# Attention, a gated layer and a soft mixture in fp32r on one core: ring tiles 32 bytes longer, with their data begun 0, 8, 16 or 24 bytes in

## The chip, the core and the metric

The kernel runs on one core of a Trainium2 chip. A core has a matrix engine (TensorE, PE in the rows; PEld is its weight loading), a vector engine (DVE), a scalar engine (ACT), GpSimd (POOL), and the queue of the sync engine (SP) that issues the DMAs. The engines run side by side and meet by semaphores. The metric is the device time of one execution in microseconds; lower is better.

## What is computed

Three layers follow one another on 2304 tokens (4 batches of 576) with 512 features. The reference, cut to what matters:

```
scores = scale * q @ k.T                      # B, H, S, D = 4, 8, 576, 64, causal
a = softmax(scores); local = a @ v
mem_out = (phi(q) @ M_prev) / (phi(q) @ z_prev + 1e-6)
x = g * mem_out + (1 - g) * local             # -> 2304 x 512

g = x @ w_gate; val = x @ w_val               # 512 x 1536 each
x = (silu(g) * val) @ w_out                   # 1536 x 512

P = exp(x @ w_gate2 - max); 8 rounds: rows to sum 1, columns to sum 1, times N/E
out = sum over 8 experts e of P[:, e] * (relu(x @ w1[e]) @ w2[e])   # 512 x 1024, 1024 x 512
```

## The kernel before

All large products are made from fp32 operands that are split in two parts of a reduced format (fp32r): `hi` is the operand copied by ACT into fp32r, `lo` is the operand less `hi`, made by DVE or POOL. A product is then three matmuls into one PSUM bank, hi·hi, hi·lo and lo·hi (`product`, L471 to L477, and the loops around L1133, L1221 and L1298). One of the two operands stands in the array (it is loaded, a LDWEIGHTS of 128 columns) and the other moves through it (256 or 512 columns). Every matmul of these products has a weight load of its own, since the order hi·hi, hi·lo, lo·hi goes through the products one by one. The load of the next matmul runs while the present one streams.

Both parts of an operand lie in one SBUF tile of a ring, `[128, 2, 512]` in fp32r, so 4096 bytes in each partition, `hi` in the first 2048 and `lo` in the second. The rings that hold such tiles, with the role of their tiles in the matmuls:

| stage | ring (name in the rows) | role | made by |
|---|---|---|---|
| gated layer, `moe1` | `xs` | moving | `split_x` L459, `halves23` L844 |
| | `gw` (8192 bytes, two such tiles) | standing | `load_units` L507, later loaded by `stream` L532 from DRAM |
| | `h` (made by `halves` L677) | moving | ACT and DVE, L679 and L680 |
| | `ws` | standing, in parts moving | `load_units`, `stream`, `unit_sums` |
| mixture, `moe2` | `xr` | moving | DMA from DRAM, L1345 |
| | `w1` (`w` in the rows) | standing | `parts` L1028 |
| | `h` (made by `split_h` L1105) | standing | ACT and DVE, L1114 to L1118 |
| | `xl` (ring of the second weights, `w2`) | moving | `parts2` L1032 |
| both | `xl` (small ring of two) | moving | `logits` L555, `parts_of` L581 |

The pool hands out places by size. In the kernel before every one of these tiles begins at a multiple of 32 bytes, and tiles of one ring stand 4096 bytes apart. Read from the built program: all `xr` tiles and all eight `h` tiles of the mixture begin 96 bytes past a multiple of 128, the ten `w1` tiles 64 past one, seven of the nine tiles of the second weights 96 past one and two of them 64. In the gated layer `gw`, `ws`, `h` and eight of eleven `xs` tiles begin 96 past a multiple of 128, three `xs` tiles 64 past.

The gated layer and the mixture use a scheme of seven products in place of eight (sums `S1` to `S4` and `T1` to `T4` of quarter matrices). In the mixture an expert's half (a "unit", 16 of them) is taken through five groups of tokens; for each, `unit_hidden` (L1120, matmuls at L1133: `pc<-xr,w` and `pt<-xr,w`, 256 columns) makes the hidden values and `unit_out` (L1277, matmuls at L1298: `pu<-xl,h` and `pq<-xl,h`, 256 columns) the output. Steps of the two are interleaved by the string "HO" * 7 (L1367), and the weights of the next unit are split beside them (`prepare_unit`). `last_hidden` (L1208, matmuls at L1221) is the short last group of tokens. In the gated layer `half` (L663, `p<-xs,gw`), `second` (L683, `po<-h,ws`) and `unit_gates` go through `product`, at L475 in the rows, mostly with 512 columns.

What sets the order: PE, ACT and DVE work in the order in which the framework's scheduler has put the instructions, and SP issues DMAs in its own order. The one stretch in which the schedule mixes two stages is the end of attention, where `load_units` turns the gated layer's weights into split tiles ahead of time.

A constant tile `ones` (L142) is filled by DVE at the start and used by `sinkhorn` (L958) alone, in the mixture's first unit.

## Time and profile before

| | |
|---|---|
| time, median of 2 runs | 2197.91 us (2197.82 to 2198.01) |
| span of the profiled execution | 2196.1 us, so 1.8 us less than the median |
| PE busy | 2149.0 us, 98% of the span, 15848 matmuls |
| PEld busy | 1960.3 us, 89% |
| DVE busy | 1679.1 us, 76% |
| ACT, POOL busy | 986.9 us (45%), 518.7 us (24%) |
| DMA | 425.77 MB, mean 194 GB/s |

Matmuls of one stream overlap: a matmul is recorded with some 280 ns, but the next one starts some 120 ns after it. So the length of a matmul's record is not its share of PE; the pace is. The pace is read from a row of the timeline that merges n matmuls of one kind: its length, less one matmul's mean length, over n - 1.

### The profile page before, as it was taken

The page shows a single profiled execution, that of the slowest core. Times are in us where ns is not written, and L with a number is a line of the kernel's source. Part 1 is how long each engine was busy: PE and PEld are TensorE (multiplying, and loading weights), DVE is VectorE, ACT ScalarE, POOL GpSimd, SP SyncE. Part 2 cuts the span into 40 slices and gives each one's busy share as a digit, 9 for nine tenths or more (in the row PEclk, how much of TensorE's full clock was granted, in tenths as well). Part 3 has the DMA queues.
Part 4 walks back from the last instruction along what each step waited for, and adds up shares of the span by engine and source line. Part 5 has one row for each costly group of instructions (what it writes and reads, how often), then busy time and mean ns, then how long its engine had stood idle before and what let it go on. Part 6 is the DMA issues. An engine that isn't in the chain of part 4 may idle for free.

```text
span 2196.1 us, 40669 instructions
## 1 busy us (share of the span) xinstructions
PE 2149.0 (98%) x15848; PEld 1960.3 (89%) x15848; DVE 1679.1 (76%) x3195; ACT 986.9 (45%) x1944; POOL 518.7 (24%) x463
## 2 busy tenths in 40 slices
PE   7999998999999899999999999999999999999999
PEld 5666677878888789999999999999999999999999
DVE  8777898675454668788887887878878788787877
ACT  6888733343333324444444444444444444444432
POOL 7766645000010042022120221202212022121100
PEclk9999999999999999999999999999999999999999
DMA  6332487466577836556465564655646556465564
GB/s 212 121 106 68 135 287 263 150 225 206 177 256 248 283 125 240 193 182 214 160 231 202 174 221 157 235 197 170 220 156 232 198 175 219 155 232 201 173 202 154
DMA packets 123359, 425.77 MB, mean 194 GB/s; under 512 B 13600, under 2 KB 13600, under 8 KB 120096
## 3 DMA queue, kind: packets, MB, share of 16 engines
q1 hardware_dynamic: 123168, 423.17, 56.5%
q8 instruction: 126, 2.06, 0.4%
q14 instruction: 65, 0.53, 0.1%
HBM read 374.36 MB, written 48.76 MB: 193 GB/s over the span
## 4 chain that ended last, share of the span: by engine, by line
PE 80%; DVE 8%; DMA 6%; issue 2%; POOL 2%; ACT 2%; SPq 1%; POOLq 0%; DVEq 0%; ACTq 0%
PE pu L1298 16%; PE pc L1133 15%; PE pq L1298 11%; PE pt L1133 11%; PE po L475 5%; PE pt L1221 4%; DMA raw<-w 4%; PE p L475 3%; PE pc L475 3%; PE po L447 2%; PE pt L475 2%; PE pq L475 2%; PE pt L414 2%; PE ps L293 1%; POOL na L504 1%
## 5 line engine op out<-in xcount | busy, mean ns | idle before, releaser
L1298 PE MATMUL pu<-xl,h 128*128 128x256 f32 x3240 | 437.3, 282 | 1.1 <-DVE xacc L1304 1.1
L1133 PE MATMUL pc<-xr,w 128*128 128x256 f32 x3072 | 408.6, 281 | 1.2 <-DVE xacc L838 0.8
L1298 PEld LDWEIGHTS pu<-xl,h 128*128 128x128 f32 x3240 | 408.4, 190 | 1.4 <-issue 1.4
L1133 PEld LDWEIGHTS pc<-xr,w 128*128 128x128 f32 x3072 | 380.8, 188 | 9.0 <-ACT m L1140 6.2
L1298 PE MATMUL pq<-xl,h 128*128 128x256 f32 x2430 | 326.4, 282 | 0.0
L1133 PE MATMUL pt<-xr,w 128*128 128x256 f32 x2304 | 306.4, 281 | 6.7 <-DVE m L1145 6.3
L1298 PEld LDWEIGHTS pq<-xl,h 128*128 128x128 f32 x2430 | 305.8, 190 | 0.1
L1133 PEld LDWEIGHTS pt<-xr,w 128*128 128x128 f32 x2304 | 285.0, 188 | 12.6 <-DVE m L1145 11.4
L1117 ACT CAST h<-m 128x512 fp32r<-128x512 f32 (+1 forms) x345 | 189.3, 557 | 217.6 <-DVE m L1149 208.0
L1304 DVE SCALAR_TENSOR_TENSOR xacc<-pu,Pw,xacc 128x256 f32<-128x256 f32 x540 | 237.9, 477 | 40.1 <-PE pu L1298 38.1
L1304 DVE SCALAR_TENSOR_TENSOR xacc<-pq,Pw,xacc 128x256 f32<-128x256 f32 x405 | 178.7, 478 | 109.9 <-PE pq L1298 109.2
L1149 DVE SCALAR_TENSOR_TENSOR m<-m 128x512 f32<-128x512 f32 x240 | 175.5, 731 | 80.7 <-ACT m L1171 79.2
L1118 DVE TENSOR_TENSOR h<-m,h 128x512 fp32r<-128x512 f32 (+1 forms) x345 | 209.3, 617 | 10.0 <-ACT h L1117 8.6
L1039 POOL TENSOR_TENSOR ws<-raw 128x512 f32<-128x512 f32 x62 | 89.0, 1447 | 520.4 <-DMA raw<-w 231.2
L1114 ACT ACTIVATE h<-m 128x512 fp32r<-128x512 f32 x192 | 121.6, 633 | 173.7 <-DVE m L1145 172.1
L1140 ACT COPY m<-pc 128x512 f32<-128x512 f32 x192 | 112.4, 586 | 186.7 <-PE pc L1133 186.6
L475 PE MATMUL p<-xs,gw 128*128 128x512 f32 (+1 forms) x864 | 172.0, 355 | 7.8 <-DVE hf L660 5.3
L475 PEld LDWEIGHTS p<-xs,gw 128*128 128x128 f32 x864 | 143.4, 189 | 34.4 <-DVE hf L660 6.9
L475 PE MATMUL po<-h,ws 128*128 128x512 f32 x576 | 144.6, 392 | 1.7 <-DVE h L680 1.2
L1026 POOL TENSOR_TENSOR w<-raw,w 128x512 fp32r<-128x512 f32 x17 | 27.5, 1620 | 476.9 <-ACT w L1025 476.9
L1115 DVE SCALAR_TENSOR_TENSOR h<-m,h 128x512 fp32r<-128x512 f32 x192 | 134.4, 700 | 4.5 <-ACT h L1114 4.3
L1145 DVE TENSOR_TENSOR m<-pt,m 128x512 f32<-128x512 f32 x192 | 131.7, 686 | 2.5 <-PE pt L1133 2.5
(244 smaller groups left out, 3004.1 us busy)
## 6 DMA issues: line engine op xcount, KB each, us to landing
xr<-xp SPq DMA_DIRECT2D x480, 512.0 KB, 4.0
raw<-w SPq DMA_DIRECT2D x64, 512.0 KB, 7.2
gw<-kg SPq DMA_DIRECT2D x24, 1024.0 KB, 6.6
graw<-gvo SPq DMA_DIRECT2D x36, 512.0 KB, 4.8
xp<-xl SPq DMA_DIRECT2D x30, 512.0 KB, 3.8
kg<-gw SPq DMA_DIRECT2D x24, 512.0 KB, 4.0
ws<-ko SPq DMA_DIRECT2D x24, 512.0 KB, 4.1
qk<-qkv SPq DMA_DIRECT2D x16, 640.0 KB, 4.1
```

Of the source, the lines that this page charges most:

```text
L475: self.nc.tensor.matmul(out, lhs[a], rhs[b], start=start and n == 0, stop=stop and n == 2, skip_group_check=shared)
L1039: op(q[name], q[a], q[b])
L1114: nc.scalar.activation(hi, src, AF.Relu)
L1115: self.later(1, lambda: nc.vector.scalar_tensor_tensor(lo, src, 0.0, f32(hi), op0=ALU.max, op1=ALU.subtract))
L1117: nc.scalar.copy(hi, src)
L1118: self.later(1, lambda: nc.vector.tensor_sub(lo, src, f32(hi)))
L1133: self.marks[3] = nc.tensor.matmul(out[:, j * HT:(j + 1) * HT], w[:, a, j, k], x[:, b, k], start=start and j + k + n == 0, stop=k + n == 3 ...
L1140: self.marks[1] = nc.scalar.copy(t, src)
L1145: nc.vector.tensor_add(t, a, b)
L1149: relu = lambda out, a, b, op: nc.vector.scalar_tensor_tensor(out, a, 0.0, b, op0=ALU.max, op1=op)
L1298: nc.tensor.matmul(po[:, c], h[a][:, x, j, c * P:(c + 1) * P], w2[b][:, y, j], start=start and c + j + n == 0, stop=j + n == 3, skip_group ...
L1304: self.marks[2] = nc.vector.scalar_tensor_tensor(acc, po[:, c], self.Pw[:, at, e:e + 1], acc, op0=ALU.mult, op1=ALU.add)
```

## The change

A new function `odd(pool, name, by)` gives a tile that is 8 elements (32 bytes) longer, and a view into it that begins `by` elements in. The rings named above take their tiles from it: `xs`, `xl` and the small `xl` ring with `by` 0, `w1` with 4 (16 bytes), `h` of the gated layer with 6 (24 bytes), `h` of the mixture with 2 (8 bytes). `wide` does the same for `gw` with 4 (16 bytes). `xr`, `ws`, `m`, `hf` and `sg` keep their tiles. So a tile of a changed ring begins 0, 8, 16 or 24 bytes past a multiple of 32, and two tiles of a ring stand 4128 bytes apart. What is computed and the tiles' shapes are as before. The tile `ones` (512 bytes) leaves the constants and is filled by POOL in `sinkhorn`'s own pool.

```diff
+def odd(pool, name, by=0):
+
+    return pool.tile([P, 2 * 512 + 8], F32R, name=name)[:, by:by + 2 * 512].rearrange("p (a n) -> p a n", a=2)
...
-        self.ones = c.tile([P, P], F32, name="ones")
-        nc.vector.memset(self.ones, 1.0)
...
-            t = (pool or self.xsp).tile([P, 2, 512], F32R, name="xs")
+            t = odd(pool or self.xsp, "xs")
...
+    def wide(self, pool):
+        t = pool.tile([P, 4 * 512 + 8], F32R, name="gw")[:, 4:4 + 4 * 512]
+        return t.rearrange("p (i a n) -> p i a n", i=2, a=2)
...
-                self.gw[f] = self.gwp.tile([P, 2, 2, 512], F32R, name="gw")
+                self.gw[f] = self.wide(self.gwp)
...
-            t = pool.tile([P, 2, 512], F32R, name="xl")[:, :, 0:m * P]
+            t = odd(pool, "xl")[:, :, 0:m * P]
...
-                t = self.xl.tile([P, 2, 512], F32R, name="xl")
+                t = odd(self.xl, "xl")
...
-                h = hp.tile([P, 2, 512], F32R, name="h")
+                h = odd(hp, "h", 6)
...
-            gws = self.stream(lambda: self.gwp, [P, 2, 2, 512], "gw", self.keptg * 2, 2)
-            wss = self.stream(lambda: wsp0, [P, 2, 512], "ws", self.kepto * 2, 3)
+            gws = self.stream(lambda: self.wide(self.gwp), self.keptg * 2, 2)
+            wss = self.stream(lambda: wsp0.tile([P, 2, 512], F32R, name="ws"), self.kepto * 2, 3)
...
+        ones = pool.tile([P, P], F32, name="ones")
+        nc.gpsimd.memset(ones, 1.0)
...
-            w1[name] = self.w1p.tile([P, 2, 2, HT], F32R, name="w1")
+            w1[name] = odd(self.w1p, "w1", 4).rearrange("p a (j n) -> p a j n", j=2)
...
-            t = self.w2p.tile([P, 2, 512], F32R, name="xl")
+            t = odd(self.w2p, "xl")
...
-        t = self.hp.tile([P, 2, 512], F32R, name="h")[:, :, 0:n]
+        t = odd(self.hp, "h", 2)[:, :, 0:n]
```

PE's instructions, with their waits, stand in the same order before and after. Two places on other engines move.

On POOL, at the border of the gated layer and the mixture's first unit (`xs` is the last split of tokens, `na` an intermediate of the weights' conversion, `ws` here the sums of quarter matrices, `w` the `w1` tiles). Before:

```order
L504 TENSOR_SCALAR na<-na 128x512 x30
L467 TENSOR_TENSOR xs<-xacc,xs 128x256 x2
L1039 TENSOR_TENSOR ws<-raw 128x512 x2
L1039 TENSOR_TENSOR ws<-ws,raw 128x512
L1039 TENSOR_TENSOR ws<-raw,ws 128x512
L1026 TENSOR_TENSOR w_6944<-raw,w_6944 128x512
```

and after:

```order
L507 TENSOR_SCALAR na<-na 128x512 x29
L470 TENSOR_TENSOR xs<-xacc,xs 128x256 x2
L969 MEMSET ones 128x128
L1049 TENSOR_TENSOR ws<-raw 128x512 x2
L1049 TENSOR_TENSOR ws<-ws,raw 128x512
L1049 TENSOR_TENSOR ws<-raw,ws 128x512
```

The fill of `ones` now stands on POOL ahead of the first unit's sums; DVE had it as its first instruction.

On DVE, at the end of attention (`gw` is the low part of a weight tile, `T` a transposed piece of attention, `xs` a split of tokens). Before:

```order
L528 TENSOR_TENSOR gw<-nb,gw 128x512
L394 TENSOR_TENSOR Z<-pt,Z 128x512
L394 TENSOR_TENSOR F<-pt,F 128x512
L528 TENSOR_TENSOR gw<-nb,gw 128x512
L488 TENSOR_SCALAR na<-na 128x512
L489 SCALAR_TENSOR_TENSOR na<-graw,na 128x512
L388 COPY xacc<-pt 128x64
L467 TENSOR_TENSOR xs<-xacc,xs 128x512
```

and after:

```order
L535 TENSOR_TENSOR gw<-nb,gw 128x512
L397 TENSOR_TENSOR Z<-pt,Z 128x512
L397 TENSOR_TENSOR F<-pt,F 128x512
L491 TENSOR_SCALAR na<-na 128x512
L492 SCALAR_TENSOR_TENSOR na<-graw,na 128x512
L470 TENSOR_TENSOR xs<-xacc,xs 128x512
L391 COPY xacc<-pt 128x64
L494 TENSOR_SCALAR nb<-na 128x512
```

Here one `gw` subtraction moves some rows down and the first `xs` split comes ahead of a copy. Such swaps go on through `load_units`, on ACT and SP too; behind it the order is as before on every engine.

## Rows read from the trace of the kernel before

**Rows 1.** The page: busy time, slices of the span, chain by engine.
```profile
PE 2149.0 (98%) x15848; PEld 1960.3 (89%) x15848; DVE 1679.1 (76%) x3195; ACT 986.9 (45%) x1944; POOL 518.7 (24%) x463
...
PEclk9999999999999999999999999999999999999999
...
PE 80%; DVE 8%; DMA 6%; issue 2%; POOL 2%; ACT 2%; SPq 1%; POOLq 0%; DVEq 0%; ACTq 0%
```

**Rows 2.** Windows: stretch, sum, busy of each engine, granted clock, DMA share, GB/s.
```profile
610.00:700.00 90.00, 86.56 (x571) 78.06 (x570) 40.98 (x70) 27.11 (x55) 9.32 (x6) 1.00 0.74 264
...
1000.00:1250.00 250.00, 249.76 (x2094) 247.94 (x2093) 200.60 (x384) 107.23 (x187) 47.38 (x31) 1.00 0.61 205
```

**Rows 3.** Whom PE waited for: total us, times, longest.
```profile
PE ps L339 <- ACT KH L254: 7.1, 1, 7.1
PE pt L1133 <- DVE m L1145: 6.3, 10, 1.3
```

**Rows 4.** Timeline of PE in the mixture: start, length, line, operation, count.
```profile
1378.04 1.57 PE L1133 MATMUL pc<-xr,w 128*128 128x256 f32 x12
1379.44 1.60 PE L1298 MATMUL pu<-xl,h 128*128 128x256 f32 x12
```

**Rows 5.** Timeline of PE in the gated layer, and in attention.
```profile
422.99 11.04 PE L475 MATMUL po<-h,ws 128*128 128x512 f32 x48
...
701.71 3.03 PE L475 MATMUL pp<-h,ws 128*128 128x256 f32 x24
```
```profile
18.07 1.56 PE L220 MATMUL po<-mask 128*128 128x128 bf16 x25
```

**Rows 6.** PE's groups by form: count, busy us, mean ns, idle before.
```profile
L1298 PE MATMUL pu<-xl,h 128*128 128x256 f32 x3240 | 437.3, 282 | 1.1 <-DVE xacc L1304 1.1
L1133 PE MATMUL pc<-xr,w 128*128 128x256 f32 x3072 | 408.6, 281 | 1.2 <-DVE xacc L838 0.8 <-ACT m L1140 0.3
L1298 PE MATMUL pq<-xl,h 128*128 128x256 f32 x2430 | 326.4, 282 | 0.0
L1133 PE MATMUL pt<-xr,w 128*128 128x256 f32 x2304 | 306.4, 281 | 6.7 <-DVE m L1145 6.3 <-DMA xr<-xp 0.2
...
L475 PE MATMUL po<-h,ws 128*128 128x512 f32 x576 | 144.6, 392 | 1.7 <-DVE h L680 1.2 <-ACT h L679 0.6
L475 PE MATMUL p<-xs,gw 128*128 128x512 f32 x576 | 134.8, 391 | 7.8 <-DVE hf L660 5.3 <-DVE sg L660 2.5
L1221 PE MATMUL pt<-xr,w 128*128 128x256 f32 x768 | 100.4, 280 | 0.0
...
L475 PE MATMUL pc<-ws 128*128 128x512 f32 x72 | 19.1, 401 | 0.0
L475 PE MATMUL pt<-xs,ws 128*128 128x512 f32 x72 | 19.1, 396 | 0.0
```

**Rows 7.** Single lines: ns of one, least/median/most, first and last start.
```profile
L1298 PE MATMUL pu<-xl,h x3240: 276/283/357, 828.8 to 2192.3; 128*128 128x256 f32 x191
```
```profile
L1133 PE MATMUL pc<-xr,w x3072: 274/280/415, 705.5 to 2162.8; 128*128 128x256 f32 x192
```
```profile
L1221 PE MATMUL pt<-xr,w x768: 274/280/288, 797.5 to 2184.2; 128*128 128x256 f32 x192
```
```profile
L475 PE MATMUL po<-h,ws x576: 387/389/501, 268.7 to 701.5; 128*128 128x512 f32 x192
```

**Rows 8.** The same for strided reads, DVE and ACT, and for an ACT cast.
```profile
L489 DVE SCALAR_TENSOR_TENSOR na<-graw,na x36: 654/679/1115, 34.6 to 385.1; 128x512 int32<-128x512 int32 x36
```
```profile
L503 ACT ACTIVATE na<-graw x36: 662/680/709, 28.1 to 376.7; 128x512 f32<-128x512 f32 x36
L490 ACT CAST gw<-na x24: 607/618/639, 238.0 to 387.4; 128x512 fp32r<-128x512 f32 x24
```

**Rows 9.** DVE's groups by form.
```profile
L1118 DVE TENSOR_TENSOR h<-m,h 128x512 fp32r<-128x512 f32 x240 | 168.8, 703 | 6.8 <-ACT h L1117 5.6
```

**Rows 10.** DMA issues: count, KB each, median us from issue to landing.
```profile
gw<-kg SPq DMA_DIRECT2D x24, 1024.0 KB, 6.6
```

More of the change, by code (lines that the diff above doesn't have):

```diff
@@ L530, in load_units, with stream @@
             yield
-    def stream(self, pool, shape, name, sources, ahead):
+    def stream(self, new, sources, ahead):
         tiles = []
@@ L537, in tile_at @@
             while len(tiles) < min(n + ahead, len(sources)):
-                tiles.append(pool().tile(shape, F32R, name=name))
+                tiles.append(new())
                 self.nc.sync.dma_start(f32(tiles[-1]), sources[len(tiles) - 1])
@@ L569, in logits @@
                 )
-        lt = f32(pool.tile([P, 2, 512], F32R, name="xl")[0:2 * E, 0])
+        lt = f32(odd(pool, "xl")[0:2 * E, 0])
         nc.vector.tensor_copy(lt[:, 0:m * P], pl[0:2 * E, 0:m * P])
@@ L856, in split @@
                 last = few.at >= 11
-                t = self.right[name, k] = few.tile([P, 2, 512], F32R, name="ws" if last else "xs")
+                t = few.tile([P, 2, 512], F32R, name="ws") if last else odd(few, "xs")
+                self.right[name, k] = t
                 nc.scalar.copy(t[:, 0], tmp[name, k])
@@ L968, in sinkhorn @@
         pt = psum.tile([P, 512], F32, name="pu")
-        nc.tensor.matmul(pt[:, 0:1], self.ones[0:1, :], m1, start=True, stop=True)
+        nc.tensor.matmul(pt[:, 0:1], ones[0:1, :], m1, start=True, stop=True)
         nm = pool.tile([P, 1], F32, name="nm")
@@ L982, in sinkhorn @@
             pt = psum.tile([P, 512], F32, name="pu")
-            nc.tensor.matmul(pt[:, 0:E], self.ones, cs, start=True, stop=True)
+            nc.tensor.matmul(pt[:, 0:E], ones, cs, start=True, stop=True)
             yield
@@ L1061, in unit_steps @@
             for n in range(4):
-                w2[n] = self.w2p.tile([P, 2, 512], F32R, name="xl")
+                w2[n] = odd(self.w2p, "xl")
                 split(w2[n], raw[:, n, 1], nc.vector)
```

## The prediction

> **What bounds the kernel now.** I read the page first. PE is busy for 98% of the span and holds 80% of the chain that ended last, and its clock is granted in full in all slices, the 2.4 GHz level [rows 1]. Then the windows by stage: near the gated layer's end PE is busy 86.56 of 90 us, in the mixture 249.76 of 250, while DVE has 200.60 of 250, ACT 107.23, and the DMA engines a share of 0.61 [rows 2]. Then the waits: the two longest that PE has come to 7.1 and 6.3 us in all [rows 3]. So from the first layer's end on, PE goes from one matmul to the next, and the time is the number of matmuls times their pace. What can move it by whole per cents is the pace.
>
> The pace is read from merged rows of the timeline. In the mixture twelve matmuls at L1133 take 1.57 us; less one of 281 ns, over eleven steps, that is 117.2 ns each. Twelve at L1298 take 1.60 us, so 119.8 ns [rows 4, 6]. In the gated layer 48 matmuls of 512 columns take 11.04 us: (11.04 - 0.392) / 47 = 226.6 ns, and 24 of 256 columns 3.03 us: 119.5 ns [rows 5, 6]. The difference, 107.1 ns for 256 columns, is the streaming itself, 0.418 ns a column. A bf16 matmul of 128 columns comes every (1.56 - 0.219) / 24 = 55.9 ns [rows 5]; its columns are 53.6 of them, and 2.3 ns are left for everything else. An fp32r matmul of 256 columns that paid no more would come every 109.4 ns, one of 512 every 216.5. So there is an excess per matmul: 10.4 ns at L1298, 7.8 at L1133, 10.1 in the gated layer. These are estimates from those rows.
>
> Is the excess a matter of place? L1133 and L1298 have one shape, one loop and the same number of columns, and differ by 2.6 ns. What differs is where their operands lie: at L1133 moving and standing tiles are 32 bytes apart modulo 64, at L1298 mostly 0. With 512 columns the mean record is 391 ns for gw with xs, 392 for ws with h, but 396 and 401 where sums of quarters (ws) stand [rows 6]. And one and the same line has records of 276 ns at the least and 283 in the middle (L1298), 274 and 280 (L1133), 387 and 389 (po) [rows 7]. So the pace does vary by some nanoseconds with something that is not the shape. That it is the place is the step that the trace leaves open, since every tile of before begins at a multiple of 32 bytes: no row has operands 8, 16 or 24 bytes apart.
>
> **The change part by part.**
>
> *The matmuls.* Touched are 3240 + 2430 = 5670 at L1298 (standing h now 8 bytes in, moving xl at 0), 3072 + 2304 + 768 = 6144 at L1133 and L1221 (standing w1 16 bytes in, xr at 0) [rows 6], and of 512 columns in the gated layer 576 + 576 = 1152 (gw against xs 16 bytes, h against ws 24) [rows 6]. Smaller groups of both lengths are left out of the sum. Unchanged in their distance within 32 bytes are the products of the sums, where ws stands and xs or ws moves.
>
> Upper bound of the gain, the whole excess: 5670 x 10.4 = 59.0, 6144 x 7.8 = 47.9, 1152 x 10.1 = 11.6, in all 119 us. The nearest rows for a matmul that meets less are the shortest records: 6 ns under the mean at L1298 (282 to 276), 7 at L1133 (281 to 274), 6 at L1221, 5 at po (392 to 387), which I take for p too. That gives 5670 x 6 = 34.0, 5376 x 7 = 37.6, 768 x 6 = 4.6, 1152 x 5 = 5.8, in all 82 us. Lower bound: the place may also cost. The worst operand pair at 512 columns is 10 ns over the best (401 against 391), and the longest record at L1221 is 8 ns over its median (288 against 280) [rows 6, 7]. At 7 ns, a little under both, for each of the 12,966 matmuls that is a loss of 91 us.
>
> I take the 82 us as the nearest, since they are records of these very lines, and give back a part: L1133 waits for DVE and ACT today by 6.3 us, and with PE 4% faster DVE's 200.60 busy us fall in 240 instead of 250; I estimate the added waits at twice today's 6.3, 12 us, of which the DMA landings in the 0.74 stretch are part. That leaves 70 us.
>
> *A rule that speaks against it.* The Trainium skill, TensorE: Matmul & The Clock Gate, Part 2, step 1, says that the matrix engine has two independent SBUF read ports, one for the moving operand and one for the weight load, so that the load of the next weights takes nothing from the running matmul. By it no distance between operands matters and the sum would be 0. The rows lean the other way, with 117.2 against 119.8 ns for one shape, but they don't prove it; it is the second case below.
>
> *DVE, ACT and POOL on tiles that begin 8 bytes in.* No row has a plain one. The nearest are strided reads that begin 4 bytes in: DVE 679 ns in the middle (L489), which is what its plain subtraction takes too (mean 703 at L1118, blocked ones among them), so 0. ACT's read at L503 takes 680 against 618 for a cast [rows 8, 9]: up to 62 ns for each of ACT's writes of h. ACT is idle for 143 of 250 us in the mixture [rows 2], and its h splits feed DVE, which waits at L1118 for only 6.8 us in 240 times; I take 0 and, if that cover were gone, 240 x 0.062 = 15 us.
>
> *DMA.* Only gw is moved by DMA while displaced: 24 loads of 1 MB, with 6.6 us to landing [rows 10], and as many stores. The loads are asked for two tiles ahead. Their least cover is at 610 to 700 us, where twelve tiles pass in 90 us, one each 7.5 us, and the DMA engines are at 0.74 [rows 2]. Bounds: 0, or, if such a load took half as long again, 3.3 us beyond a cover of 7.5 x 2 - 6.6 = 8.4, so still hidden; at double the engines would fill up, and I put that at 1 us for each of 12, 12 us. I take 0.
>
> *The order.* The fill of `ones` leaves DVE's head and stands on POOL ahead of the first unit's sums; its neighbours there take over 1 us each on an engine that is 24% busy [rows 1], and `sinkhorn` wants it much later: 0. Behind it on POOL are only those sums. The swaps of gw subtractions, copies and xs splits on DVE lie in the last stretch of attention; they put the same instructions up to a few rows later, at 0.7 us a row [rows 9]. PE's order and waits don't change. 0, bounds -3 to +3 us.
>
> **Sum.** 2196.1 + 1.8 = 2197.9, the median; less 70 us: **2128 us**, 3.2% less.
>
> **The rivals.**
> - *The places decide little.* Either the two read paths do not meet, as the rule has it, or they meet as often at 8 and 16 bytes as at 0 and 32, because the streams run through all places in any case and only the moment of the meeting shifts. For it: no row shows a displacement under 32, and the step from 0 to 32 goes with 2.6 ns only. Then 2198 us, from 2160 to 2230.
> - *The places cost.* A stream that begins inside a 32-byte piece touches one piece more at its end, or falls in with the weight load more often; it is one price for each matmul. At 3.4 ns a matmul it passes 2% (44 us / 12,966), at 7 ns it is 91 us: 2289. For it: pairs with 396 and 401 ns exist. Against it: the lines touched are now nearer to their worst than to their best (L1298 282, 283 in the middle, of 276 at the least).
> - *All of the excess goes*, in the small groups left out too, which would add some us to the 119: about 2071. Against it: the give-back above.
>
> **How the numbers follow.** Forecast with its own range of 2071 to 2154: 0.53. Little: 0.32. Cost, over 2242: 0.13; the rest are gains beyond the forecast's range. A gain or loss of under 2%, which is about what a measurement of this kernel can tell from no change, covers 2154 to 2242. Faster by over 2%: 0.53, within 2%: 0.33, slower: 0.14. The range takes in the forecast's gains and the larger part of the second case: 2070 to 2215.
>
> **What would show it.** Right: the same rows of the timeline give under 115 ns at L1298 and L1133, the mean records fall to 276 to 278 (256 columns) and 385 to 388 (512), the number of matmuls in a 250 us window of the mixture rises from 2094 to some 2165, and PE's waits for DVE grow a little. DVE's and ACT's mean lengths and the 6.6 us of the gw loads stay. Wrong: records of 282 as before (second case); of 286 and more (third); or shorter records, with PE idle before L1133 by tens of us, which would say that DVE has become the bound.

## The result, and the profile after

| | before | after |
|---|---|---|
| time, median | 2197.91 us | 2213.74 us (2211.90 to 2215.59) |
| ratio to before, with its 95% interval | | 1.0077 (1.0055 to 1.0098) |
| span of the profiled execution | 2196.1 us | 2210.1 us |
| pace at L1298, now L1308 | 119.1 ns | 118.3 ns |
| pace at L1133, now L1143 | 117.3 ns | 118.6 ns |
| pace of `p<-xs,gw`, 512 columns | 227.3 ns | 231.4 ns |
| pace of `po<-h,ws`, 512 columns | 228.2 ns | 233.5 ns |

The change makes the kernel 0.8% slower; the forecast was 3.2% less. A pace here, and in all that follows, is the mean time from one matmul's start to the next over the whole trace, steps with a wait (over 1.25 times the median) left out.

The page of the changed kernel, its busy time, granted clock and chain, answers to [rows 1]:

```profile
PE 2161.9 (98%) x15848; PEld 1964.9 (89%) x15848; DVE 1682.0 (76%) x3194; ACT 986.9 (45%) x1944; POOL 521.0 (24%) x464
...
PEclk9999999999999999999999999999999999999999
...
PE 84%; DVE 6%; DMA 4%; POOL 2%; issue 2%; ACT 2%; SPq 0%; POOLq 0%; DVEq 0%; ACTq 0%
```

PE is as full as before, and its clock is granted at 0.9 or more in every slice, as before. Its windows answer to [rows 2]: the mixture has 2088 matmuls in 250 us where it had 2094, and not the 2165 of the forecast. (The first window holds other matmuls than before, since all work there stands some 15 us later.)

```profile
610.00:700.00 90.00, 87.22 (x526) 75.62 (x525) 43.55 (x73) 30.65 (x61) 10.83 (x9) 0.98 0.76 265
1000.00:1250.00 250.00, 249.87 (x2088) 247.97 (x2088) 203.69 (x392) 105.97 (x187) 50.69 (x33) 1.00 0.59 198
```

The timeline and the groups by form answer to [rows 4 to 6]. By the first row of `po` a matmul comes every (11.36 - 0.399) / 47 = 233.2 ns, where it was 226.6; twelve at L1143 take 0.01 us more than before, twelve at L1308 0.02 less. No record mean falls to 276 or 385; those of the 512-column groups rise from 391 and 392 to 399, single records of up to 768 ns among them; the median of `po` goes from 389 to 395.

```profile
437.50 11.36 PE L478 MATMUL po<-h,ws 128*128 128x512 f32 x48
...
1395.82 1.58 PE L1143 MATMUL pt<-xr,w 128*128 128x256 f32 x12
1397.24 1.58 PE L1308 MATMUL pq<-xl,h 128*128 128x256 f32 x12
```
```profile
L1308 PE MATMUL pu<-xl,h 128*128 128x256 f32 x3240 | 434.7, 281 | 1.1 <-DVE xacc L1314 1.1
L1143 PE MATMUL pc<-xr,w 128*128 128x256 f32 x3072 | 412.1, 282 | 2.5 <-DMA xr<-xp 1.3 <-DVE xacc L845 0.8 <-ACT m L1150 0.3
...
L478 PE MATMUL po<-h,ws 128*128 128x512 f32 x576 | 149.2, 399 | 2.9 <-ACT h L686 1.5 <-DVE h L687 1.4
L478 PE MATMUL p<-xs,gw 128*128 128x512 f32 x576 | 139.9, 399 | 12.1 <-DVE hf L667 6.7 <-ACT hf L666 3.0 <-DVE sg L667 2.3
```

**Where the time went.** PE's instructions stand in one order in all kernels here, so the n-th matmul's start can be set against its start before. The table gives the delay, in us, of the matmul that starts at the given time in the trace of before; the rows behind the first are experiments below.

| | 241 us | 335 | 460 | 730 | 1300 | 2190 |
|---|---|---|---|---|---|---|
| the change | 0.5 | 8.1 | 15.3 | 15.2 | 15.3 | 14.0 |
| e14, gw 32 bytes longer, nothing displaced | -0.1 | 7.0 | 14.2 | 15.5 | 14.5 | 13.3 |
| e2, the change with gw 64 bytes longer | -0.1 | -1.8 | 0.6 | 2.2 | 4.4 | 1.1 |
| e4, the change in the mixture alone | -0.1 | -1.8 | -1.8 | -1.1 | 3.9 | 0.8 |
| e12, the best pair of places in the mixture | 0.6 | -0.3 | -0.1 | -0.9 | -4.1 | -12.6 |

In the profiled executions all of the loss arises between 241 and 460 us: in the end of attention and the first stage of the gated layer, while `load_units` converts the weights. From there on the changed kernel is as fast as the old one, with 84% of the matmuls still to come. The windows of that stretch, first of before, then of the change (same columns): PE does 930 matmuls in 219 us before, 866 after, with 208.4 and 202.6 us busy.

```profile
241.00:335.00 94.00, 87.73 (x402) 70.25 (x401) 87.93 (x149) 43.83 (x79) 53.46 (x26) 1.00 0.77 258
335.00:460.00 125.00, 120.64 (x528) 97.26 (x527) 92.14 (x159) 45.55 (x77) 25.84 (x12) 1.00 0.54 186
```
```profile
241.00:335.00 94.00, 86.86 (x377) 67.67 (x378) 80.21 (x135) 40.07 (x72) 54.10 (x26) 0.96 0.70 236
335.00:460.00 125.00, 115.78 (x489) 90.36 (x488) 92.35 (x153) 44.47 (x76) 28.74 (x14) 1.00 0.55 191
```

What the stretch from 241 to 460 us adds can be split step by step, each step set against the same one of before, in us:

| | steps with a wait of PE | steps within a spell of low clock | all other steps | sum |
|---|---|---|---|---|
| the change | 6.8 | 2.8 | 5.2 | 14.8 |
| e14 | 8.4 | 1.4 | 4.5 | 14.3 |
| e2 | -4.5 | 1.5 | 3.7 | 0.7 |
| e4 | -2.9 | 1.5 | -0.4 | -1.8 |

The other steps that grow are those of 512 columns. In a spell the clock is granted at its lower level, 1.2 GHz, where it is 2.4 GHz otherwise. The change has two spells here (hence 0.96 in its row from 241 us), e14, e2 and e4 have one, before none. Each of the five begins within 1 us behind a wait of PE of 2.1 to 4.0 us; before has such waits, of 2.2 and 2.8 us, without a spell. Spells don't explain the loss: e4 has one and loses nothing, and e14 loses nearly as much as the change with one less. Between the change and e2, which has the old order, the waits differ by 11.3 us, the spells by 1.3 and the other steps by 1.5.

Who waits there, ACT in the window from 241 to 460 us, before and after (total, times, longest):

```profile
ACT ws L490 <- DVE na L489: 21.1, 9, 4.3
```
```profile
ACT ws L493 <- DVE na L492: 37.9, 11, 5.4
...
ACT na L506 <- DVE nb L496: 15.2, 5, 4.3
ACT gw L493 <- DMA kg<-gw: 12.7, 8, 6.9
```

The conversion runs from engine to engine (ACT, POOL, DVE, ACT, DVE, DMA) through rings of three or four tiles. After the change ACT's cast into a gw tile waits 12.7 us for the store of the tile's former contents, ahead of it in the ring, and the conversion's first step on ACT (L506) waits 15.2 us for DVE's work on nb; before, the first wait isn't in ACT's list for this window, and the second is its eighth, 3.8 us. The stores themselves don't take longer, 3.5 us in the median from issue to landing where it was 4.0; they are issued later. The second of the 24 goes out at 250.9 us, where it was 241.5, and the last at 411.7, where it was 393.8; e14 has 250.3 and 411.0, and e2, in the old order, 241.4 and 390.3. Behind those casts on ACT and DVE stand `hf` and `xacc`, and these are what PE waits for in this stretch, for 16.0 us in all, where it was 10.6 before (5.3 `hf`, 2.8 `xacc`, 2.5 `sg`); before, then after:

```profile
PE p L475 <- DVE hf L660: 5.3, 4, 1.6
PE pt L414 <- DVE xacc L388: 2.8, 1, 2.8
PE p L475 <- DVE sg L660: 2.5, 2, 2.2
```
```profile
PE p L478 <- DVE hf L667: 6.7, 6, 2.1
PE pt L417 <- DVE xacc L391: 4.0, 1, 4.0
PE p L478 <- ACT hf L666: 3.0, 2, 1.5
PE p L478 <- DVE sg L667: 2.3, 3, 1.1
```

### The profile page after: what moved, and what is told of

It is laid out like the page before. It is cut to its first block, busy times and chain, and to the rows that moved or that the text cites. A ratio compares the mean times of both kernels' runs of the same rounds, so it can differ in the third digit from the quotient of the medians.

```text
span 2210.1 us, 40640 instructions
## 1 busy us (share of the span) xinstructions
PE 2161.9 (98%) x15848; PEld 1964.9 (89%) x15848; DVE 1682.0 (76%) x3194; ACT 986.9 (45%) x1944; POOL 521.0 (24%) x464
## 4 chain that ended last, share of the span: by engine, by line
PE 84%; DVE 6%; DMA 4%; POOL 2%; issue 2%; ACT 2%; SPq 0%; POOLq 0%; DVEq 0%; ACTq 0%
PE pu L1308 16%; PE pc L1143 16%; PE pq L1308 12%; PE pt L1143 12%; PE po L478 5%; PE pt L1231 4%; PE pc L478 3%; PE p L478 3%; PE pt L478 2%; PE po L450 2%; DMA raw<-w 2%; PE pq L478 2%; PE pt L417 2%; POOL na L507 2%; PE ps L296 1%
## 5 line engine op out<-in xcount | busy, mean ns | idle before, releaser
L1308 PE MATMUL pu<-xl,h 128*128 128x256 f32 x3240 | 434.7, 281 | 1.1 <-DVE xacc L1314 1.1
L1143 PE MATMUL pc<-xr,w 128*128 128x256 f32 x3072 | 412.1, 282 | 2.5 <-DMA xr<-xp 1.3
L1308 PEld LDWEIGHTS pu<-xl,h 128*128 128x128 f32 x3240 | 405.5, 188 | 1.5 <-issue 1.5
L1143 PEld LDWEIGHTS pc<-xr,w 128*128 128x128 f32 x3072 | 383.3, 188 | 10.6 <-ACT m L1150 6.5
L1308 PE MATMUL pq<-xl,h 128*128 128x256 f32 x2430 | 324.1, 281 | 0.0
L1143 PE MATMUL pt<-xr,w 128*128 128x256 f32 x2304 | 308.5, 282 | 3.5 <-DVE m L1155 3.3
L1308 PEld LDWEIGHTS pq<-xl,h 128*128 128x128 f32 x2430 | 303.2, 188 | 0.1
L1143 PEld LDWEIGHTS pt<-xr,w 128*128 128x128 f32 x2304 | 287.3, 188 | 8.5 <-DVE m L1155 7.5
L1128 DVE TENSOR_TENSOR h<-m,h 128x512 fp32r<-128x512 f32 (+1 forms) x345 | 209.6, 618 | 8.5 <-ACT h L1127 7.0
L478 PE MATMUL p<-xs,gw 128*128 128x512 f32 (+1 forms) x864 | 176.6, 360 | 12.1 <-DVE hf L667 6.7
L478 PE MATMUL po<-h,ws 128*128 128x512 f32 x576 | 149.2, 399 | 2.9 <-ACT h L686 1.5
L478 PEld LDWEIGHTS po<-h,ws 128*128 128x128 f32 x576 | 108.7, 191 | 29.9 <-DVE h L687 2.4
```

The lines of the kernel that those rows point to most:

```text
L478: self.nc.tensor.matmul(out, lhs[a], rhs[b], start=start and n == 0, stop=stop and n == 2, skip_group_check=shared)
L1128: self.later(1, lambda: nc.vector.tensor_sub(lo, src, f32(hi)))
L1143: self.marks[3] = nc.tensor.matmul(out[:, j * HT:(j + 1) * HT], w[:, a, j, k], x[:, b, k], start=start and j + k + n == 0, stop=k + n == 3 ...
L1308: nc.tensor.matmul(po[:, c], h[a][:, x, j, c * P:(c + 1) * P], w2[b][:, y, j], start=start and c + j + n == 0, stop=j + n == 3, skip_group ...
```

## The experiments

All kernels below but the probes have `ones` in `sinkhorn`'s pool, as the change has. Each probe was run once. The theories in short: A, two losses, by the order of the weights' conversion and by the pace of 512 columns; B, where operands begin causes all of it, or decides nothing (each text says which); C, the rings' longer pitch; D, the distance between operands counts; M, the moving operand's place; A2 and P, each pair of places has its own pace; T, changes of tiles keep the pace from settling; N, neighbours on other engines do. "Places" are given as (standing, moving), in bytes modulo 64. In the probes a moving tile is named by its place and a standing one by w and its place: `bank<-fortyeight,weight` has (8, 48).

**What of the change costs: e2, e3, e4, e14.** e2, against the changed kernel:

```
-        t = pool.tile([P, 4 * 512 + 8], F32R, name="gw")[:, 4:4 + 4 * 512]
+        t = pool.tile([P, 4 * 512 + 16], F32R, name="gw")[:, 4:4 + 4 * 512]
```

> The changed kernel, but gw tiles are 64 bytes longer and not 32; all data begin 0, 8, 16 or 24 bytes in as in the change. With this length the weights' conversion and its stores stand in the order of the kernel before (but for six rows on DVE). Theory A (two losses: some 9 us by the order of the conversion, 5 to 6 us by the pace of 512 columns, the mixture a gain of 1): 2203 us, 2201 to 2206, and PE's delay against the kernel before at 455 us is 5 us and not 15. Theory B (all of the loss comes from where the operands begin): 2213. Theory C (the longer pitch of the rings): 2213.

Measured: 2201.1 us, ratio 1.0021 (1.0010 to 1.0032), against the change's 1.0077. So 0.56%, 12.3 us (7 to 18), go by the order of the conversion, and at 460 us the delay is 0.6 us. PE does 927 matmuls in the 219 us:

```profile
241.00:335.00 94.00, 90.47 (x408) 71.90 (x407) 87.70 (x149) 43.74 (x79) 60.25 (x26) 1.00 0.77 264
335.00:460.00 125.00, 121.81 (x519) 97.02 (x518) 92.14 (x157) 45.58 (x77) 24.30 (x12) 0.99 0.51 180
```

e3 has the change's tiles with all data begun at 0, `odd(..., 0)` and `[:, 0:4 * 512]`:

> The changed kernel with all data begun at 0 in the longer tiles: the pitch and the order of the change, no odd multiple of 8 bytes; distances are 0 or 32 modulo 64. Theory A: the order's loss of 9 us stays, the 512-column pace loses 0 to 5 us (partly locked), so 2206 to 2213 us. Theory B: 2198. Theory C: 2213.

Measured: 2208.4 us, 1.0056 (1.0043 to 1.0070). Most of the loss is there without any odd multiple of 8 bytes. `p<-xs,gw` has 232.7 ns, so the length alone takes the 512 columns out of their 227 ns too.

e4 leaves the gated layer as before and keeps the change in the mixture (`h` by 2, `w1` by 4 elements, second weights and small `xl` ring longer):

> Only the mixture's rings (h 8 bytes in, w1 16 bytes in, second weights and the small xl ring at 0) are longer; the gated layer's xs, gw and h are as in the kernel before, and so is the order up to the gated layer's end. Theory A: the mixture's own net, a gain of 1 us: 2197 (2195 to 2199), L1308 at 118.3 ns where it was 119.1, L1143 at 118.5 where it was 117.3. Theory B: the same by the trace, since the loss lies in the gated layer. The prediction's step: 2130.

Measured: 2198.3 us, 1.0007 (0.9997 to 1.0016); L1308 118.3 ns, L1143 118.5. The one gains 0.8 x 5670 = 5 us, the other loses 1.2 x 6144 = 7. So in the mixture, where the forecast put 76 of its 82 us, the change does nothing that shows.

e14 is the kernel before with gw alone 32 bytes longer, and nothing displaced:

```
-                self.gw[f] = self.gwp.tile([P, 2, 2, 512], F32R, name="gw")
+                self.gw[f] = self.wide(self.gwp)
...
+        t = pool.tile([P, 4 * 512 + 8], F32R, name="gw")[:, 0:0 + 4 * 512]
```

> Of all rings only gw has longer tiles, by 32 bytes as in the change, and its data begin at 0: nothing is displaced, all other rings lie as before. The weights' conversion takes the order of the change. Theory A (order): 2196.7 + 12 us (the changed kernel less e2_gw64) + 2 us (gw tiles lie 0 and 32 by turns, so that half of the 512-column products leave 227 ns): 2210 us (2206 to 2213). Theory B (displacement): 2198. Theory D of e10 (only the pace): 2200.

Measured: 2212.9 us, 1.0076 (1.0064 to 1.0088), the whole loss of the change, and its delays, within 1.2 us, at every point of the table. In this kernel ACT's casts wait 13.4 us for the stores, and on DVE the first subtraction into a gw tile that moves stands nine rows later, behind pieces of attention:

```profile
241.00:335.00 94.00, 85.58 (x377) 66.53 (x376) 81.04 (x136) 39.42 (x71) 54.25 (x24) 0.98 0.69 236
335.00:460.00 125.00, 115.25 (x489) 90.10 (x488) 91.96 (x152) 44.54 (x77) 27.45 (x13) 1.00 0.54 190
```
```profile
ACT gw L493 <- DMA kg<-gw: 13.4, 8, 7.9
```

With gw 64 bytes longer the trace shows the old order, but for a few rows (e2) or in full (e10), with 32 the new one; what makes the scheduler choose wasn't found. The chain from late subtraction to late store to late cast is read from the waits and the stores' times; no run moves one row alone.

**What a place is worth: p1, p5, p7.** The probe's core, 48 matmuls for each pair of places:

```
for r in range(4):
    for k in range(4):
        for a, b in ((0, 0), (0, 1), (1, 0)):
            nc.tensor.matmul(out, w[a][:, k * P:(k + 1) * P], x[b][:, j:j + n], ...)
```

> A probe: TensorE alone, none of the layers is computed. 48 fp32r matmuls with a weight load each (hi.hi, hi.lo, lo.hi, four blocks, four times) for each of 16 distances between the start of the moving and of the standing operand, 0 to 60 bytes past a multiple of 64 in steps of 4, with 256 and with 512 columns, then again in the opposite order, and then with the lo part 8, 16 or 32 bytes further from hi than 2048. Theory A (the distance modulo 64 bytes sets the pace, by whether the starts lock): at distance 0 a matmul every 120.0 ns (256 columns) and 226.7 (512); at 32 about 117.2 and 231; at 8, 16 and 24 between 117.5 and 119 and 231 to 233; none under 116 and 225. Theory B (the distance decides nothing, and the paces of the kernel come from its neighbours on other engines): all 16 within 0.5 ns of each other. The prediction's step: 112 to 114 ns and 221 to 223 at 8, 16 and 24.

Timeline of p1, 256 columns, standing at 0 and moving at 0, 4, 8 and 12 (start, length, line, operation, count):

```profile
27.27 5.93 PE L68 MATMUL bank<-zero,w 128*128 128x256 f32 x48
33.08 6.14 PE L68 MATMUL bank<-four,w 128*128 128x256 f32 x48
39.10 6.01 PE L68 MATMUL bank<-eight,w 128*128 128x256 f32 x48
44.99 5.85 PE L68 MATMUL bank<-twelve,w 128*128 128x256 f32 x48
```

The lengths differ, with no other engine at work: 123.3 ns at 4, 120.0 at 8, 116.7 at 12, and 118.6 in the first turn, 120.0 in the second, at 0 (mean of the steps from the seventh on; the first step behind the small matmul takes some 200 ns). With 512 columns 228.9 at 12, 238 to 240 at 4 and 20, 231 to 234 at 8, 16 and 24. The prediction's step has 112 to 114 and 221 to 223 at 8, 16, 24, and falls; so does theory B. Theory A misses too with 512 columns: at distance 0, where it had 226.7, the probe has 232.4. Here the standing operand stays at 0, so distance and place of the moving operand are one. p5 takes them apart:

> A probe as p1_places, TensorE alone, no layer computed: with 256 columns all pairs of 16 starts of the standing operand (0 to 60 bytes past a multiple of 64, in steps of 4) and 16 of the moving one; with 512 columns the 16 starts of the moving one against standing starts 0, 4, 16 and 32; then 256 columns with the lo parts 0 to 56 bytes further off. Theory A1 (only the distance counts): each diagonal of the grid has one pace within 1 ns, with the lowest at distances of 12, 28, 44 and 60, at 116.3 to 117.8 ns (256) and 229 to 230 (512), the highest at 4 and 20, at 122 to 123 and 238 to 240. Theory A2 (the place of each operand within its 64 bytes counts): paces on a diagonal spread by 3 ns and more, and 512 columns with both operands 32 bytes past a multiple of 64, as in the kernel before, give its 226.7 and not the 232.4 of p1_places.

The diagonals of the 16 x 16 grid are not alike; theory A1 falls. The mean over all standing places is 118.2 to 118.8 ns for a moving operand at 0, 16, 32, 48, then 121.1 to 121.5 at 4, 20, 36, 52, then 120.3 to 121.1 at 8, 24, 40, 56, and 117.4 to 118.3 at 12, 28, 44, 60. The mean over all moving places goes from 118.8 to 120.0 only, that over a diagonal from 118.7 to 120.1. So the place of the moving operand modulo 16 counts most: it makes 57% of the variance over the 256 pairs, the distance 5% and the standing place 3%; the rest lies in single pairs. Of the operands that the change displaces, all but the gated layer's `h` are standing ones. Single pairs go further, (8, 48) and (56, 16) to 113.3; whether this was chance, p7 asks:

> A probe as p1_places and p5_grid, TensorE alone, no layer computed: 20 pairs (standing, moving) of places modulo 64 with 256 columns, each begun six times at another moment (behind a small matmul of 128, 117, 106 columns and so on), then 11 pairs with 512 columns begun three times, and there also products whose moving operand changes between 0 and 32 from block to block, as it does where the tiles of one ring stand 4128 bytes apart. Theory A2 (a pair of places has a pace of its own, whatever the moment): the six starts agree within 0.5 ns; pairs (8,48) and (56,16) at 113.3 again, (32,32) at 120.0; 512 columns 226.7 at (0,0), (32,32), (16,0) and (16,32), 233 at (32,0) and (0,32), and 231 to 233 where the moving operand changes. Theory A3 (the moment decides as much as the place): single pairs spread by 3 ns and more over the six starts; then no choice of places gives 113.3 in a kernel that changes tiles every 6 to 12 matmuls.

In 17 of the 20 pairs the six starts agree within 0.5 ns; (0, 32) goes from 116.6 to 117.8, (16, 32) from 117.3 to 120.0, (8, 32) from 117.8 to 123.3. Rows of p7: (32, 32), which L1298 mostly had, (40, 32), and (8, 48) at its first and its second start:

```profile
33.12 5.99 PE L68 MATMUL bank<-thirtytwo,wthirtytwo 128*128 128x256 f32 x48
...
80.41 5.81 PE L68 MATMUL bank<-thirtytwo,wforty 128*128 128x256 f32 x48
86.21 5.71 PE L68 MATMUL bank<-fortyeight,weight 128*128 128x256 f32 x48
...
203.78 5.71 PE L68 MATMUL bank<-fortyeight,weight 128*128 128x256 f32 x48
```

0.28 us over 47 steps are 6.0 ns: 119.9, 115.6 and 113.3. Theory A2 holds for these 17 pairs, which have a pace of their own within one probe; three show two paces. With 512 columns 227 at (0, 0) and (32, 32), 226.7 at (16, 32), 233.3 at (32, 0) and (0, 32), and 230 to 235 where the moving operand changes between 0 and 32 from block to block, as in rings of 4128 bytes. (16, 0) had 226.7 in p5 and 233.3 here, and (0, 0), at 227 here, had 232.4 in p1, where other tiles lay between the two. So the pair of places modulo 64 doesn't always fix the pace; what else does wasn't found.

**Does the kernel follow? e6, e8, e9, e10, e11, e12.** e6 is e4 with `h` and `w1` 4 bytes in:

> Mixture only, gated layer as before, as in e4_mixture_only, but h and w1 begin 4 bytes in (e4: 8 and 16), so that the moving operand lies 60 or 28 bytes past the standing one modulo 64, where p1_places has its lowest paces. Theory A: L1308 falls to 116.5 ns a matmul (119.1 before) and L1143 to 116.5 (117.3 before): 5670 x 2.6 + 6144 x 0.8 = 20 us less than the kernel before, 2178 us (2172 to 2186). Theory B (in the kernel the neighbours blur it, and places decide nothing): 2198 us, as e4. The give-back of the prediction (DVE late) would show as waits of PE at L1143, some us.

Measured: 2201.8 us, 1.0024 (1.0014 to 1.0033), L1308 118.7 ns, L1143 118.7: a miss of 24 us. The expectation rested on the distance, before p5 was read; both displaced operands stand, and the moving ones remain at 0 and 32. e8 and e9 displace the moving one alone (the small `xl` ring keeps its 32 bytes more, with its data at 0):

```
-            t = odd(self.w2p, "xl")
+            t = odd(self.w2p, "xl", 3, 8)     # e8: 12 bytes; e9: 1, 4 bytes
```

> Of all rings only that of the second weights (xl, moving at L1308) has longer tiles, and its data begin 12 bytes in; h and w1 of the mixture and the whole gated layer lie as in the kernel before. Theory M (what counts is where the moving operand begins, modulo 16, as the columns of p5_grid have it: 118.5 ns at 0, 121.4 at 4, 120.6 at 8, 117.7 at 12): L1308 at 117.7, 5670 x 1.4 = 8 us less, 2190 us (2186 to 2194). Theory D (the distance between the two operands counts, as the prediction had it): distances are 12 and 44, where the diagonals of p5_grid average 119.9: 2201.

> As e8_moving_12, but the second weights begin 4 bytes in. Theory M: L1308 at 121.4 ns, 5670 x 2.3 = 13 us more, 2211 us (2205 to 2216). Theory D: distances 4 and 36, diagonals of 120.1 and 119.4: 2201. Theory B (places decide nothing): 2198, as e8.

Measured: e8 2193.9 us, 0.9991 (0.9980 to 1.0002); e9 2209.8, 1.0062 (1.0048 to 1.0077). One and the same edit, 8 bytes apart, and the second 0.7% slower; the groups of e8, then of e9, show it at L1308, 117.7 and 121.0 ns a step:

```profile
L1308 PE MATMUL pu<-xl,h 128*128 128x256 f32 x3240 | 432.6, 279 | 1.1 <-DVE xacc L1314 1.1
```
```profile
L1308 PE MATMUL pu<-xl,h 128*128 128x256 f32 x3240 | 443.7, 284 | 1.1 <-DVE xacc L1314 1.1
```

Theory M holds for L1308 in both. e8 gained 2 us and not 8, not told from nothing, since L1143 has 118.2 here, 0.9 ns more for each of 6144 matmuls. `w1`, not displaced, lies 96 bytes from `xr` modulo 128 where it was 32; that this is the cause wasn't tested by itself.

> Of all rings only gw has longer tiles (64 bytes, so that the order of the conversion stays that of the kernel before), its data begin 16 bytes in, 48 modulo 64 where they stood at 32; xs stays at 32. Theory M: a standing operand may lie anywhere, the loss of the 512-column products in the change came from the moving operand, whose tiles lie 0 and 32 by turns in rings of 4128 bytes and at 24 in the gated layer's h: p<-xs,gw stays at 227 ns, 2198 us (2196 to 2200). Theory D: 231 to 232 ns, 864 x 4.5 = 3 to 4 us more, 2201.

Measured: 2198.5 us, 1.0013 (1.0001 to 1.0025), `p<-xs,gw` at 232.2 ns. Theory M fails here: with 512 columns the standing place counts, and D's pace came (the time, 2.8 us over before by the ratio, fits both). The next two give the mixture's tiles 128 bytes more, so that all tiles of a ring lie alike:

> e4_mixture_only once more, with the same places of the data in their tiles (h 8 bytes in, w1 16), but tiles 128 bytes longer and not 32, so that all tiles of a ring lie alike modulo 128. The pairs (standing, moving) modulo 64 are then (40,32) in 4590 of the 5670 matmuls at L1308, (40,0) in the rest, (16,32) at L1143. Theory P (each pair of places has its own pace, and the 32 bytes mixed good and bad pairs): by p7_starts 115.6, 119.1 and 117.3 ns, so L1308 at 116.4 where it was 119.1 before the change: 5670 x 2.7 = 15 us less, 2183 us (2178 to 2192). Theory B (in the kernel tiles change every 6 to 12 matmuls, and the pace of a pair is lost): 2198, as e4.

Measured: 2198.8 us, 1.0006 (0.9995 to 1.0017). L1308 fell to 117.6 ns, not 116.4, and L1143 rose to 119.1, so nothing is left.

```
+            w1[name] = odd(self.w1p, "w1", 10, 32).rearrange("p a (j n) -> p a j n", j=2)
...
+            t = odd(self.w2p, "xl", 4 if self.w2p.at % 9 < 7 else 12, 32)
...
+        t = odd(self.hp, "h", 26, 32)[:, :, 0:n]
```

> As e11_same_by_128, with the places that have the lowest paces in p7_starts: h begins 104 bytes in and the second weights 16 or 48, which makes the pair (8,48) of all matmuls at L1308, and w1 40 bytes in, (40,32) at L1143. The gated layer is as in the kernel before. Theory P: 113.3 ns at L1308 and 115.6 at L1143 and L1231: 5670 x 5.8 + 6144 x 1.7 = 43 us less, 2155 us (2148 to 2170), with PE's waits for DVE at L1143 a few us up. Theory B: 2198.

Measured: 2184.4 us, 0.9940 (0.9925 to 0.9955), the fastest here: 13 us less than before, a third of what was expected. L1308 has 116.8 ns, L1143 117.4; the window of the mixture has 2114 matmuls:

```profile
1000.00:1250.00 250.00, 249.78 (x2114) 247.82 (x2113) 202.16 (x387) 108.54 (x189) 47.05 (x31) 1.00 0.60 208
```

In e12 the steps within a group of twelve at L1308, averaged over the groups, fall from 118.8 and 117.6 ns, the first two, to 115.0, the tenth and eleventh, where the pair alone has 113.3.

**Why the kernel doesn't reach the pace of its pair: p13, e15, e16.** p13 has groups of twelve by turns, as at L1143 and at L1308 (27 pairs for the latter), and no other engine:

> A probe, TensorE alone, no layer computed: groups of twelve matmuls of 256 columns as at L1143 (moving at 32, standing at one of 16 places) and as at L1308 (one of 28 pairs of places) by turns, four of each, and at the end 512 columns with hi and lo of the standing operand 4096 bytes apart as in gw, at six places modulo 128. Theory T (the pace settles only within some matmuls of a change of tiles, so groups of twelve don't reach the pace of their pair): without any other engine the probe shows the kernel's paces, mean of both kinds: 118.2 ns for the places of the kernel before ((32,32) with (0,32)), 117.1 for e12_best_pair ((8,48) with (40,32)), 118.3 for e11_same_by_128 ((40,32) with (16,32)), within 0.5 ns. Theory N (neighbours hold the matmuls in the kernel): the probe shows the means of the pairs' own paces, 118.3, 114.5 and 116.5. With 512 columns: 226.7 at 96 as in the kernel before; at 48 and 112 231 to 233 if the place modulo 128 explains e10_gw_only, 226.7 if it doesn't.

The places of before, then of e12, then (40, 32) for both (`hidden` as L1143, `outer` as L1308):

```profile
4829.19 1.59 PE L68 MATMUL outer<-thirtytwo,wthirtytwo 128*128 128x256 f32 x12
4830.61 1.57 PE L68 MATMUL hidden<-thirtytwo,wzero 128*128 128x256 f32 x12
```
```profile
329.52 1.57 PE L68 MATMUL outer<-fortyeight,weight 128*128 128x256 f32 x12
330.93 1.56 PE L68 MATMUL hidden<-thirtytwo,wforty 128*128 128x256 f32 x12
```
```profile
880.39 1.55 PE L68 MATMUL hidden<-thirtytwo,wforty 128*128 128x256 f32 x12
881.78 1.55 PE L68 MATMUL outer<-thirtytwo,wforty 128*128 128x256 f32 x12
```

The places of before give 117.2 and 119.5 ns (L1143 and L1308; the first turn of each is left out), the kernel 117.3 and 119.1. Those of e12 give 116.6 and 117.3, where the pairs alone have 115.6 and 113.3; the kernel has 117.4 and 116.8. So for e12 the change of tiles alone takes most of the gain, without neighbours, as theory T has it. The places of before can't tell the theories apart (118.2 against 118.3). For e11 the probe has 116.8 in the mean, close to theory N's 116.5, and the kernel 118.3: a miss of theory T. With 512 columns, in the way gw lies, 226.8 ns at 96 modulo 128, 231.9 at 48 and 233.3 at 112, which explains e10's 232.2. e15 and e16 are two of the lowest choices of p13, 115.6 and 115.0 ns (`h`, `w1` and second weights moved as in e12, by other amounts):

> As e12_best_pair, other places: h and w1 begin so that both lie at 40 modulo 64, and all second weights at 32, as xr does; the pair is (40,32) for all matmuls of 256 columns in the mixture. Theory T (the probe by twelves holds in the kernel): 115.6 ns at L1143 and at L1308, with no settling between groups: 6144 x 1.7 + 5670 x 3.5 = 30 us less, 2166 us (2160 to 2174). Theory N (neighbours keep the kernel's pace over 116.8, the lowest so far): 2184, as e12, or more.

> As e15_40_and_40 with h and w1 at 44 and the second weights at 16 modulo 64: (44,16) at L1308, (44,32) at L1143. Theory T: 113.3 and 116.7 ns as in the probe by twelves: 5670 x 5.8 + 6144 x 0.6 = 37 us less, 2160 us (2154 to 2168). Theory N: 2184 or more.

Measured: e15 2186.7 us, 0.9956 (0.9939 to 0.9973); e16 2187.4, 0.9960 (0.9945 to 0.9975). L1308 and L1143 have 117.3 and 117.3 ns in e15, 117.5 and 117.2 in e16. Both are faster than before, and both miss the probe by some 2 ns in the mean of the two lines, at L1308 of e16 by 4.2. In the probe the steps of (40, 32) are 117, 115, 115 without end; in e15 a third of the steps stand in such triples, in short pieces. So theory T isn't all of it. What breaks the pattern in the kernel (waits of single matmuls, the half-length groups between, a neighbour) stays open.

## Why the prediction was wrong

- **What bounds the kernel**: right for the mixture. PE is full there, the time is matmuls times pace, and e9 and e12 moved the time by the pace alone. The loss came where PE does wait, in the stretch from 241 to 460 us.
- **The matmuls, 82 us: the step that failed.** It took the shortest single records (276, 274, 387) as the length that all records would have once operands are displaced. In the kernel before they are its short steps (at L1298 a record's length goes with the step behind it, correlation 0.87), not the pace of another distance. Records of 277 ns in the mean do occur, at 113.3 ns for (8, 48) in p7, but the change makes no such pair. And it took the distance between operands for what counts; the probes show the place of the moving operand modulo 16 and then the single pair, and the change displaced standing operands, at 8 and 16 bytes. In the mixture, where the term was a gain of 76 us, e4 measures a loss of 1.5 (-0.7 to 3.5). In the gated layer the step went the wrong way: the 10.1 ns of excess there was already the low state (227; in p5 59 of 64 pairs have 228.8 to 240), and the change left it, 231.4 and 233.5.
- **The hint that L1298 and L1133 differ by place**: right, and the probes confirm it: (32, 32) 119.9, (0, 32) 116.7 ns. It was read as a sign of a large effect beyond; it is about the size of the largest gain found here, 2.3 ns at L1308 in e12.
- **The rule set against it.** The Trainium skill, TensorE: Matmul & The Clock Gate, Part 2, step 1, has two independent read ports, and taken as the prediction takes it, no place matters. The runs don't agree that no place matters: 113.3 to 122.4 ns for one shape in p7, and 226.8 to 233.3 in p13 where only the standing operand's place differs. Whether the two reads share a port, they don't show. But for this change its rival's 2198 us is what the mixture did.
- **The order, 0 with bounds of 3 us: the second step that failed**, by a factor of four (12.3 us, the change less e2; with the 512-column pace of gw tiles that lie 0 and 32 by turns, 16.7 us, e14). The rows moved were priced by their own 0.7 us. What counts is the ring behind them: a late subtraction makes a late store, ACT's cast waits for the store, and attention's and the gated layer's work on ACT and DVE stands behind that cast. PE waits there for DVE already before: [rows 6] have 5.3 us for `hf` and 2.5 for `sg`, which shows how little slack there is.
- **DVE, ACT and POOL on displaced tiles, 0; the loads of gw, 0**: right. The split at L1128 takes 705 ns in the mean for 703 [rows 9], the cast into gw 619 for 618 in the middle [rows 8], a load of gw 6.7 us for 6.6 [rows 10].
- **The rivals.** "The places cost" had the sign, but not the mechanism. A begin inside a 32-byte piece is no price by itself: in p5 a moving operand at 12 modulo 16 has 117.7 ns, at 0 118.5. At 512 columns the cost is 4 to 5 ns for some 1500 matmuls, 7 us by the paces and 3 by the ratios of e2 and e4, and with 256 columns one line's loss meets the other's gain. That a change of a tile's length moves the schedule was no rival at all, though the order of DVE in that stretch stood in the text. The measured 2213.7 us lies within the range of 2070 to 2215 by luck: the upper part was meant for places that decide little, and most of the loss came by the order.

By the ratios, the change's 0.77% are 0.56 for the order (the change less e2), 0.14 for the gated layer's paces (e2 less e4), 0.07 for the mixture (e4). The last two aren't told from nothing by the times; the gated layer's paces are by the traces.

## What to carry to other kernels

Where PE is full, measure a supposed effect of place alone, in a probe of fifty matmuls for each pair of places, before pricing it by the shortest records of a trace. A lengthened tile changes more than the address: see whether the scheduler has put the work around its ring in another order, and price the order by the waits through the ring, not by the rows moved. And a pace that a pair of places has in a long run need not be that of a kernel that changes tiles every twelve matmuls.

## What was not expected of the hardware

Back-to-back fp32r matmuls with a weight load each have a pace that depends on the places of both operands, repeatably within 0.5 ns in 17 of 20 pairs of p7: with 256 columns from 113.3 ns, (8, 48) and (56, 16), to 123.4 and once 126.7, with 512 from 226.7 to 240.0. With 256 columns most of it goes by where the moving operand begins modulo 16 bytes: 12 is best with 117.7 ns in the mean of p5, 4 worst with 121.4. A place modulo 128 counts too: gw at 96 and 32 has 226.8 and 229.0 ns in p13, at 80 and 16 226.7 and 230.0. After a change of tiles the pace settles late: in p13, with the places of e12, the steps of (40, 32) do from the sixth on, and in e12 those of (8, 48) are still at 115.0 at the eleventh.
